# Block-sparse attention, Fourier mixing and an MLP in one kernel: from the tenth head pair on, DMAs turn q, k and the selection mask, and TensorE sums k's blocks

## The chip, the cores and the metric

The kernel runs on one core of one Trainium2 chip. Its time is the device time of one execution in microseconds. Before the change three runs gave 328.68, 330.34 and 330.57 us; the median is 330.34 us. Five engines work beside each other, each through its own instructions in order: TensorE (PE; its weight loads are PEld), VectorE (DVE), ScalarE (ACT), GpSimd (POOL) and SyncE (SP), which here only issues DMAs.

## The reference

Inputs are q, k and v of 4 batches, 8 heads, 768 positions and 64 channels, and two weight matrices. For each head the 768 keys form 12 blocks of 64. A query is scored against the mean key of each block (the gate), keeps the three best blocks that aren't in its future and its own block, and attends to their keys causally. The attention output goes through a two-dimensional Fourier transform over positions and channels, whose real part is added to it; then come a normalisation over the channels and an MLP.

```python
k_rep = k.reshape(B, H, n_blocks, block, D).mean(axis=3)
gate_scores = np.einsum('bhsd,bhnd->bhsn', q, k_rep)
gate_scores = np.where(causal, gate_scores, -1000000000.0)
top_idx = np.argsort(gate_scores, axis=-1)[..., -top_k:]
# mask: the three best blocks and the own block, and causal
scores = np.where(mask, scale * np.matmul(q, k.transpose(0, 1, 3, 2)), -1000000000.0)
out = softmax(scores) @ v
...
X = np.fft.fft(np.fft.fft(x, axis=1), axis=2)
u = x + np.real(X)
un = (u - mean(u)) / np.sqrt(var(u) + 1e-06)
return u + np.maximum(un @ w_ch1, 0.0) @ w_ch2
```

Only the order of the gate scores matters, but it must be right in float32, since a swapped block changes the output.

## The kernel before, in words

Work goes by pairs of heads: `kk` = 0 to 15, four pairs to a batch. Each pair has a slot of six parts (`p` = 0 to 5) in the main loop (L748 to L797). What a slot does for its own pair and for the next two is written out by hand: `USUAL` and `NORM` (L746, L747) name the part in which each stage stands. The order on TensorE and GpSimd is the program's order (`manual_schedule`, L679); a scheduler orders DVE, ACT and SP by its own estimate of when each instruction is ready.

The stages, by the lines that the prediction speaks of:

- `load_qk`, `load_v` (L213, L227): SP loads q, k and v of a pair, two DMAs each, some pairs ahead.
- `stage_A` (L266), in slot `kk` for pair `kk+2`: TensorE transposes q and k by 128x128 blocks in float32 (L281, 12 to a pair). Before pair 8 q goes to float32 (`qT`) and GpSimd casts it to the f16 operand `qg` (L242); from pair 8 on (`SPLIT`) ACT makes the f16 high part of 64 q (L289), DVE the remainder (L290), and GpSimd copies the high part. DVE sums k's columns by blocks (L294) and splits the sums in two f16 parts (L306, L307). ACT copies k to the f16 operand `kI` (L313).
- `stage_B` (L318), in part 5 of the same slot: the gates. Up to pair 7 five float32 matmuls (L325), from pair 8 on ten f16 ones (L333); then DVE adds the causal constants, finds the third largest of each row (L342) and writes the selection `gmp`.
- `stage_C` (L352), in part 3 of the slot after: TensorE transposes the selection (L356, five), DVE copies it to rows 64 to 75 of `qg` (L359). `kI` holds a constant in those rows (-60000 at a key's own block), so that the score matmul over 76 rows adds the mask.
- `stage_S` (L378): scores (L388) and exponential (L393), for both heads `e` and three sections `s` each: six to a slot, one to a part. From pair 7 on DVE masks the diagonal after it (L399).
- `stage_AV` (L401): output (L414) and division by the row sum (L419, L420).

After a batch's fourth pair its Fourier stages (`stage_S1`, L488 to L499; `stage_S2`, L515 to L529), the normalisation (`stage_N`, L545 to L562), a turn of its result (`stage_T`: SP's transposing DMA L570 for batches 1 and 2 and a part of 3, else TensorE L574) and the MLP (`stage_M1`, L589 to L594; `stage_M2`, L603 to L607) are put between the stages of later pairs as units by `filler` (L654), a planner that spreads units over the half parts by a credit. A unit of the Fourier chain stands where its due time by the planner's own clock (`feed.now`) says; that clock runs on the costs handed to `main` and on the units' costs. The last batch's chain and MLP have no pair left to stand beside; they make up the end.

PSUM tiles come from four buffers of one bank ("ps") and two of two banks for the scores ("sc").

In the profile a slot is the stretch from the first score matmul of its pair (L388) to that of the next.

Of the kernel before, what the change touches and what calls it, by code (L numbers as in the profile page):

```python
# [19 lines left out]
def _consts_np():  # L20
# [30 lines left out]
    IndN = np.where(nn[:, None] == (s[None, :] // 64), NEG, 0.0).astype(np.float16)  # L51
    return dict(CS=CS, SS=SS, CD=CD, SDN=SDN, SDP=SDP, ident32=ident32, ident16=ident16,
                ut01=ut01, ltri=ltri, cz24=cz24, oth24=oth24, IndN=IndN)
# [65 lines left out]
def kernel(  # L119
# [65 lines left out]
    kI_t = [[const([128, S], F16, f"kI_{e}_{sl}") for sl in range(3)] for e in range(2)]  # L185
    v16_t = [const([128, 2, NST, 66], F16, f"v16_{sl}") for sl in range(4)]
    qg_t = [[const([128, S], F16, f"qg_{e}_{sl}") for sl in range(3)] for e in range(2)]
    warm = const([128, 512], F16, "warm")
    kr24_t = [const([128, 2 * NB], FP, f"kr24_{sl}") for sl in range(2)]
    krx_t = [const([128, 2, 2 * NB], F16, f"krx_{sl}") for sl in range(2)]  # L190
# [11 lines left out]
    SPLIT = 8  # L202
# [32 lines left out]
    def cast_v(kk):  # L235
        P[kk]["v16"] = v16_t[kk % 4]
        nc.gpsimd.tensor_copy(out=v16_t[kk % 4][:, :, :, 0:64], in_=P[kk]["vn"])

    def cast_q(kk):
        d = P[kk]  # L240
        for e in range(2):
            nc.gpsimd.tensor_copy(out=d["qg"][e][0:64, :],  # L242
                                  in_=d["qt" if kk < SPLIT else "qh"][64 * e:64 * e + 64, :])

# [21 lines left out]
    def stage_A(kk, who, g):  # L266
        d = P[kk]
        src = d["qn"] if who == 0 else d["kn"]
        if who == 0 and g == 0:
            d["qt"] = apool.tile([128, S], FP, tag="qT32", name=f"qT32_{kk}")  # L270
            if kk >= SPLIT:
                parts = d["qt"].bitcast(F16)
                d["qh"], d["ql"] = parts[:, 0:S], parts[:, S:2 * S]
            d["qg"] = [qg_t[e][kk % 3] for e in range(2)]
        if who == 1 and g == 0:
            d["kI"] = [kI_t[e][kk % 3] for e in range(2)]
            d["kr12"] = spool.tile([128, NB], FP, tag="kr12", name=f"kr12_{kk}", bufs=2)
            d["kr24"] = kr24_t[kk % 2]
# [6 lines left out]
        if who == 0:  # L285
            if kk < SPLIT:
                (nc.scalar.copy if kk == LATE else nc.vector.tensor_copy)(out=d["qt"][:, cols], in_=flat)
            else:
                nc.scalar.activation(out=d["qh"][:, cols], in_=flat, func=AF.Copy, scale=QS)  # L289
                STT(out=d["ql"][:, cols], in0=flat, scalar=QS, in1=d["qh"][:, cols], op0=MULT, op1=SUB)  # L290
            if g == 1 and kk != LATE:
                cast_q(kk)
        else:
# [3 lines left out]
            if g == 1 and kk < SPLIT:  # L297
# [3 lines left out]
            elif g == 1:  # L301
                d["krx"] = krx_t[kk % 2]
                for e in range(2):
                    r, c = slice(64 * e, 64 * e + 64), slice(NB * e, NB * (e + 1))
                    hi, lo = d["krx"][r, 0, c], d["krx"][r, 1, c]
                    nc.vector.tensor_scalar(out=hi, in0=d["kr12"][r, :], scalar1=QS, scalar2=None, op0=MULT)  # L306
                    STT(out=lo, in0=d["kr12"][r, :], scalar=QS, in1=hi, op0=MULT, op1=SUB)  # L307
            for e in range(2):
                dst, src_ = d["kI"][e][0:64, cols], flat[64 * e:64 * e + 64]
                if kk < EARLY and g == 1 and e == 1:  # L310
                    nc.vector.tensor_copy(out=dst, in_=src_)
                else:
                    nc.scalar.copy(out=dst, in_=src_)  # L313

# [3 lines left out]
    def stage_B(kk):  # L318
# [9 lines left out]
        else:  # L328
            gps = pst([128, NG, 2, 2 * NB], f"g_{kk}")
            krx = d["krx"].rearrange("p o n -> p (o n)")  # L330
            for st in range(1, NST):
                for n, part in enumerate((d["qh"], d["ql"])):
                    nc.tensor.matmul(gps[:, st - 1, :, :].rearrange("p o n -> p (o n)"),  # L333
                                     part[:, 128 * st:128 * (st + 1)], krx, start=(n == 0), stop=(n == 1))
            nc.vector.tensor_tensor(out=gsf, in0=gps[:, :, 0, :], in1=cz24[:, 1:NST, :], op=ADD)
            nc.vector.tensor_tensor(out=gsf, in0=gps[:, :, 1, :], in1=gsf, op=ADD)
# [12 lines left out]
        else:  # L349
            STT(out=gm, in0=gm, scalar=QS, in1=oth24[:, 1:NST, :, :], op0=MULT, op1=MULT)  # L350

    def stage_C(kk):  # L352
# [5 lines left out]
        for e in range(2):  # L358
            nc.vector.tensor_copy(out=d["qg"][e][64:64 + NB, 128:S],  # L359
                                  in_=gt[32 * e:32 * e + NB].rearrange("p a c -> p (a c)"))  # L360
# [17 lines left out]
    def stage_S(kk, e, s):  # L378
        d = P[kk]
        if s == 0:  # L380
            d.setdefault("pt", {})[e] = apool.tile([128, 3 * SEC], F16, tag=f"ptl{e}",
                                                   name=f"ptl_{kk}_{e}")
# [3 lines left out]
        for (jt, a0, a1, co) in SECS[s]:  # L386
            diag = by_pe and a0 == 128 * jt
            nc.tensor.matmul(sp[:, co:co + (a1 - a0)],  # L388
                             d["kI"][e][0:76, 128 * jt:128 * (jt + 1)],
                             d["qg"][e][0:76, a0:a1], start=True, stop=not diag)  # L390
            if diag:
                nc.tensor.matmul(sp[:, co:co + 128], id16, ltri, start=False, stop=True)  # L392
        nc.scalar.activation(out=pt[:, SEC * s:SEC * (s + 1)], in_=sp[:, 0:SEC], func=AF.Exp,  # L393
                             scale=0.125 if kk < SPLIT else 0.125 / QS)
# [284 lines left out]
    with tc.manual_schedule(engines={mybir.EngineType.PE, mybir.EngineType.Pool}):  # L679
# [12 lines left out]
        for t in krx_t:  # L692
            nc.gpsimd.memset(t, 0.0)
        for t in gmp_t:
            nc.vector.memset(t, 0.0)
        for sl in range(3):
            for e in range(2):
                nc.gpsimd.dma_start(kI_t[e][sl][64:64 + NB, :], dr["IndN"].ap())
        nc.gpsimd.dma_start(ut01, dr["ut01"].ap())
        for e in range(2):  # L700
            for sl in range(3):
                nc.gpsimd.memset(qg_t[e][sl][64:64 + NB, 0:128], 0.0)
        load_v(0)
        for sl in range(4):
# [43 lines left out]
        for kk in range(NK):  # L748
            at = NORM if kk == NORM_SLOT else USUAL
            for p in range(6):  # L750
# [9 lines left out]
                if p == 1 and kk - 1 == NORM_SLOT:  # L760
                    main(stage_B, 0.35, kk + 1)
                if p == at["A1"] and kk + 2 < NK:
# [67 lines left out]
```

## Time and profile before

| what | value |
|---|---|
| three runs | 328.68, 330.34, 330.57 us |
| the profiled execution: its own time / its span | 330.56 us / 328.8 us |
| clock granted to TensorE, mean over the span | 0.995 |
| busy: PE, DVE, ACT, POOL | 309.1, 229.8, 179.9, 84.3 us |
| starts of slots 6 to 15 | 75.8, 86.9, 106.0, 124.8, 142.5, 162.1, 179.5, 197.6, 216.3, 234.5 us |
| last exponential of slot 15 | 249.6 us |
| longest total of PE's own waits with a named releaser | 3.4 us (scores on the exponential) |

How to read it. Times in a view are microseconds from the span's start; "L603" is line 603 of the kernel. The page gives each engine's busy time, the span in 40 slices of 8.2 us with the busy share in tenths, and the chain of work that ended last. A group line names line, engine, operation, out<-in, count, then busy time and mean duration in ns, then the idle time before it and who ended it. A mean duration holds the pipeline's depth: matmuls start one behind another at a fraction of it, and the chain of waits shows what each adds. SPq lines are the times in which SP issues a DMA. A wait line says who waited for whom, with total, count and longest.

### The profile page before, as it was taken

How to read it: one execution, taken by the hardware profiler on the slowest of the kernel's cores; microseconds unless marked ns; L12 is line 12 of the kernel's file. 1: busy time of each engine (PE TensorE's matmuls, PEld its weight loads, DVE VectorE, ACT ScalarE, POOL GpSimd, SP SyncE). 2: the span in 40 equal slices, each digit the busy share in tenths (PEclk: the TensorE clock that was granted, in tenths of full speed). 3: DMA queues.
4: the chain of work that ended last, by engine and by line, in shares of the span. 5: the costliest groups of instructions: out<-in, count | busy, mean ns of one | idle time of the engine just before them, and what ended most of it. 6: DMA issues, size and time to landing. Idle time of an engine off the chain costs nothing.

```text
span 328.8 us, 6922 instructions
## 1 busy us (share of the span) xinstructions
PE 309.1 (94%) x2656; PEld 199.5 (61%) x2656; DVE 229.8 (70%) x736; ACT 179.9 (55%) x276; POOL 84.3 (26%) x137
## 2 busy tenths in 40 slices
PE   7799998997799999998999999997999999999994
PEld 3577776976566667654666776553666654566442
DVE  3778879489786898998667889995357588433211
ACT  3178888598976766446595856345564302244000
POOL 8444573540464030505041131302030000000000
PEclk9999998899999999999999999999999999999999
DMA  8995989992499642434733000114100011200021
GB/s 201 244 260 135 268 129 227 155 208 50 98 181 202 114 98 50 140 85 114 190 76 74 0 2 35 45 53 96 66 0 2 0 67 70 90 3 0 34 96 64
DMA packets 92929, 33.02 MB, mean 100 GB/s; under 512 B 85352, under 2 KB 88752, under 8 KB 92896
## 3 DMA queue, kind: packets, MB, share of 16 engines
q1 hardware_dynamic: 87600, 27.71, 34.5%
q0 software_dynamic: 3552, 4.40, 8.8%
q10 hardware_dynamic: 1744, 0.46, 0.6%
q8 instruction: 21, 0.34, 0.4%
q14 instruction: 12, 0.10, 0.1%
HBM read 28.63 MB, written 6.29 MB: 106 GB/s over the span
## 4 chain that ended last, share of the span: by engine, by line
PE 68%; DVE 19%; ACT 7%; DMA 2%; issue 2%; ACTq 0%; DVEq 0%
PE ch L603 19%; PE ha L589 15%; PE hb L589 8%; PE sc L388 7%; PE av L414 4%; ACT ptl L393 3%; ACT kI L313 3%; PE g L325 3%; PE za L488 2%; PE tp L281 2%; DVE mx L342 2%; DVE kr L294 2%; DVE bst L528 2%; DVE ptl L399 2%; DVE u L526 2%
## 5 line engine op out<-in xcount | busy, mean ns | idle before, releaser
L393 ACT ACTIVATE ptl<-sc 128x896 f16<-128x896 f32 x96 | 87.3, 918 | 43.9 <-PE sc L388 34.4
L603 PE MATMUL ch<-w_sb,hT 128*128 128x512 f16 x384 | 91.2, 379 | 0.9 <-DVE qT L290 0.9
L589 PEld LDWEIGHTS <-w_sb 128*128 128x128 f16 x512 | 48.6, 97 | 37.7 <-issue 3.8
L589 PE MATMUL ha<-unT,w_sb 128*128 128x512 f16 x256 | 65.7, 379 | 0.6 <-DMA unT<-x 0.5
L603 PEld LDWEIGHTS <-hT 128*128 128x128 f16 x384 | 36.4, 97 | 36.3 <-issue 0.8
L388 PE MATMUL sc<-qg,kI 76*128 76x512 f16 (+3 forms) x256 | 55.0, 307 | 3.4 <-ACT ptl L393 3.4
L592 ACT ACTIVATE hT<-ha 128x512 f16<-128x512 f32 x64 | 38.1, 598 | 30.7 <-PE ha L589 30.5
L594 DVE TENSOR_SCALAR hT<-hb 128x256 f16<-128x256 f32 x64 | 26.7, 420 | 30.3 <-PE hb L589 30.2
L589 PE MATMUL hb<-unT,w_sb 128*128 128x256 f16 x256 | 38.4, 272 | 1.7 <-DMA unT<-x 1.6
L434 POOL TENSOR_TENSOR fs<-x 128x384 f16<-128x384 f16 x12 | 10.9, 909 | 106.7 <-DVE x L420 91.9
L388 PEld LDWEIGHTS <-kI 76*128 76x128 f16 x256 | 24.1, 100 | 19.5 <-issue 2.6
L313 ACT CAST kI<-tp 64x384 f16<-64x384 f32 x57 | 27.0, 474 | 14.6 <-DVE kr L294 13.5
L606 DVE TENSOR_TENSOR u<-ch,u 128x512 f32<-128x512 f32 x24 | 16.4, 683 | 19.6 <-PE ch L603 19.3
L414 PEld LDWEIGHTS <-ptl 128*128 128x128 f16 x672 | 24.1, 97 | 3.1 <-DVE ptl L399 0.4
L414 PE MATMUL av<-v,ptl 128*128 128x65 f16 x672 | 25.7, 193 | 0.1
L294 DVE TENSOR_REDUCE kr<-tp 128x6 f32<-128x384 f32 x32 | 17.0, 549 | 8.2 <-PE tp L281 8.0
L561 ACT ACTIVATE x<-u,nmr,rstd 128x512 f16<-128x512 f32 x12 | 8.9, 804 | 18.8 <-issue 17.0
L392 PE MATMUL sc<-ltri,id 128*128 128x128 f16 x84 | 18.6, 222 | 0.0
L420 DVE TENSOR_TENSOR x<-av,rcp 128x384 f16<-128x384 f32 x32 | 17.8, 556 | 1.0
L399 DVE TENSOR_TENSOR ptl<-ptl,ut 128x384 f16<-128x384 f16 x36 | 13.8, 419 | 5.7 <-ACT ptl L393 5.7
L528 DVE BATCH_NORM_STATS2 bst<-u 128x6 f32<-128x512 f32 x24 | 16.6, 692 | 1.2 <-ACT u L524 0.7
L359 DVE COPY qg<-gt 12x640 f16<-12x640 f16 x32 | 15.5, 484 | 2.0 <-PE gt L356 1.1
(115 smaller groups left out, 408.2 us busy)
## 6 DMA issues: line engine op xcount, KB each, us to landing
vn<-in_v_dram SPq DMA_DIRECT2D x32, 192.0 KB, 3.6
out_dram<-u SPq DMA_DIRECT2D x24, 256.0 KB, 2.0
kn<-in_k_dram SPq DMA_DIRECT2D x30, 192.0 KB, 3.4
qn<-in_q_dram SPq DMA_DIRECT2D x30, 192.0 KB, 3.3
w_sb<-in_moe_w_ch_dram POOLq DMA_DIRECT2D x8, 256.0 KB, 7.0
w_sb<-in_moe_w_ch_dram POOLq DMA_DIRECT2D x4, 512.0 KB, 8.8
cs_sb<-c_CS SPq DMA_DIRECT2D x1, 289.5 KB, 4.6
ss_sb<-c_SS SPq DMA_DIRECT2D x1, 289.5 KB, 4.8
```

Source lines behind the costliest of these rows:

```text
L294: nc.vector.tensor_reduce(out=d["kr12"][:, 6 * g:6 * g + 6], in_=ps.rearrange("p a (x c) -> p a x c", x=2), axis=mybir.AxisListType.X, op=ADD)
L313: nc.scalar.copy(out=dst, in_=src_)
L388: nc.tensor.matmul(sp[:, co:co + (a1 - a0)], d["kI"][e][0:76, 128 * jt:128 * (jt + 1)], d["qg"][e][0:76, a0:a1], start=True, stop=not diag)
L392: nc.tensor.matmul(sp[:, co:co + 128], id16, ltri, start=False, stop=True)
L393: nc.scalar.activation(out=pt[:, SEC * s:SEC * (s + 1)], in_=sp[:, 0:SEC], func=AF.Exp, scale=0.125 if kk < SPLIT else 0.125 / QS)
L399: nc.vector.tensor_tensor(out=dg, in0=dg, in1=um, op=MULT)
L414: nc.tensor.matmul(av[:, st, 0:65], pt[:, o:o + 128], d["v16"][:, e, jt, 0:65], start=(cnt == 0), stop=(cnt == 20))
L528: nc.vector.bn_stats(out=bst, in_=u_b[:, kt, :])
L589: nc.tensor.matmul(hp_, w1_sb[:, dt, 128 * it:128 * (it + 1)], unT[:, dt, c0:c1], start=(dt == 0), stop=(dt == NDT - 1))
L592: nc.scalar.activation(out=hT[:, c0:c1], in_=hp_, func=AF.Relu)
L594: nc.vector.tensor_scalar(out=hT[:, c0:c1], in0=hp_, scalar1=0.0, scalar2=None, op0=mybir.AluOpType.max)
L603: nc.tensor.matmul(cps, x["hT"][it][:, 128 * st:128 * (st + 1)], w2_sb[:, it, :], start=(it == 0), stop=(it == NIT - 1))
```

## The change

It sets `SPLIT` to 9 and replaces the path of pairs 9 to 15, in three steps.

1. `split(kk+2)`, where `stage_A` of q stood (part 2): from the loaded float32 q and k, ACT writes the high f16 part of 64 q and 64 k (two instructions over 768 columns), DVE the remainders (640 and 768 columns), all with positions on the partitions. Two transposing DMAs of 12 blocks of 128x128 each, on SP, turn q's two parts into `qhl` and k's high part with the constant rows into `kI`. There are no transposes on TensorE for these pairs, no block sums on DVE and no copies of q on GpSimd.
2. `stage_R(kk+2)`, where `stage_B` stood (part 5): 24 matmuls of two columns, with 64-column weights from k's high and low part and an indicator as the moving operand, sum k's blocks in PSUM. DVE splits the sums in two f16 parts, ACT copies both to partitions 64 to 127.
3. `stage_B(kk+1)` moves to part 1 of the slot after, with ten f16 matmuls of 24 columns. DVE writes the selection into the low part's columns of `qs`, and a third transposing DMA turns `qs` into `qg`, mask rows included. `stage_C` goes.

Pair 8 goes back to the float32 path. `kI` and `qg` hold both heads in one tile with 128-column blocks of the two in turn; `v16` has three buffers in place of four, the exponentials' tiles one per head in place of two. In slot 3 SP loads the constant columns and GpSimd clears the unused ones. The costs that `main` hands the planner follow (transposes 1.4 less to a slot, gates 0.3, block sums 0.6).

```diff
-    SPLIT = 8
+    SPLIT = 9
...
+    def turn(dst, src):
+        nc.sync.dma_start_transpose(dst.rearrange("p s e c -> p (s e) c"),
+                                    src.rearrange("p s e c -> p (s e c)"))
+
+    def split(kk):
+        d = P[kk]
+        kn, qn = d["kn"], d["qn"]
+        d["qs"] = qs = qs_t[kk % 2]
+        d["qhl"] = apool.tile([128, S], FP, tag="qT32", name=f"qhl_{kk}").bitcast(F16).rearrange(
+            "p (s e c) -> p s e c", e=2, c=128)
+        khi, qhi = ks[:, :, :, 0:64], qs[:, :, :, 0:64]
+        nc.scalar.activation(out=qhi, in_=qn, func=AF.Copy, scale=QS)
+        STT(out=qs[:, 1:NST, :, 64:128], in0=qn[:, 1:NST, :, :], scalar=QS, in1=qhi[:, 1:NST, :, :],
+            op0=MULT, op1=SUB)
+        turn(d["qhl"], qs)
+        nc.scalar.activation(out=khi, in_=kn, func=AF.Copy, scale=QS)
+        turn(kI_t[kk % 3], ks)
+        STT(out=klo, in0=kn, scalar=QS, in1=khi, op0=MULT, op1=SUB)
+        d["kI"], d["qg"] = kI_t[kk % 3], qg_t[kk % 3]
+
+    def stage_R(kk):
+        d = P[kk]
+        d["krs"] = krs = krs_t[kk % 2]
+        rps = pst([64, 2, NB], f"r_{kk}")
+        for st in range(NST):
+            for e in range(2):
+                o = rps[:, e, 2 * st:2 * st + 2]
+                nc.tensor.matmul(o, ks[:, st, e, 0:64], ind2, start=True, stop=False)
+                nc.tensor.matmul(o, klo[:, st, e, :], ind2, start=False, stop=True)
+        hi, lo = krs[0:64, :, 0, :], krs[0:64, :, 1, :]
+        nc.vector.tensor_copy(out=hi, in_=rps)
+        nc.vector.tensor_tensor(out=lo, in0=rps, in1=hi, op=SUB)
+        nc.scalar.copy(out=krs[64:128, :, :, :], in_=krs[0:64, :, :, :])
...
-            gps = pst([128, NG, 2, 2 * NB], f"g_{kk}")
-            krx = d["krx"].rearrange("p o n -> p (o n)")
+            gps = pst([128, NG, 2, 2, NB], f"g_{kk}")
             for st in range(1, NST):
-                for n, part in enumerate((d["qh"], d["ql"])):
-                    nc.tensor.matmul(gps[:, st - 1, :, :].rearrange("p o n -> p (o n)"),
-                                     part[:, 128 * st:128 * (st + 1)], krx, start=(n == 0), stop=(n == 1))
+                for e in range(2):
+                    nc.tensor.matmul(gps[:, st - 1, e, :, :].rearrange("p o n -> p (o n)"),
+                                     d["qhl"][:, st, e, :],
+                                     d["krs"][:, e, :, :].rearrange("p o n -> p (o n)"), start=True, stop=True)
...
-            STT(out=gm, in0=gm, scalar=QS, in1=oth24[:, 1:NST, :, :], op0=MULT, op1=MULT)
+            STT(out=d["qs"][:, 1:NST, :, 64:64 + NB], in0=gm,
+                scalar=QS * QS, in1=oth24[:, 1:NST, :, :], op0=MULT, op1=MULT)
+            turn(qg_t[kk % 3], d["qs"])
...
-                if p == 1 and kk - 1 == NORM_SLOT:
-                    main(stage_B, 0.35, kk + 1)
-                if p == at["A1"] and kk + 2 < NK:
+                if p == 1 and (kk - 1 == NORM_SLOT or SPLIT <= kk + 1 < NK):
+                    main(stage_B, 0.3 if kk + 1 >= SPLIT else 1.05, kk + 1)
+                if p == at["A1"] and kk + 2 < min(SPLIT, NK):
                     main(stage_AA, 0.7, kk + 2, 1)
-                if p == at["C"] and kk + 1 < NK:
+                if p == at["C"] and kk + 1 < min(SPLIT, NK):
                     main(stage_C, 0.3, kk + 1)
...
                 if p == at["A0"]:
                     if kk + 2 < NK:
-                        main(stage_AA, 0.7, kk + 2, 0)
+                        if kk + 2 < SPLIT:
+                            main(stage_AA, 0.7, kk + 2, 0)
+                        else:
+                            split(kk + 2)
...
                 if p == at["B"] and kk + 2 < NK:
-                    main(stage_B, 1.05 if kk + 2 < SPLIT else 0.35, kk + 2)
+                    if kk + 2 < SPLIT:
+                        main(stage_B, 1.05, kk + 2)
+                    else:
+                        main(stage_R, 0.6, kk + 2)
...
+            if kk == 3:
+                nc.gpsimd.memset(ks[:, :, :, 64 + NB:128], 0.0)
+                for t in qs_t:
+                    nc.gpsimd.memset(t[:, 0, :, 64:128], 0.0)
+                for e in range(2):
+                    nc.sync.dma_start(ks[:, :, e, 64:64 + NB],
+                                      dr["IndT"].ap().rearrange("(st p) n -> p st n", p=128))
+                    nc.gpsimd.memset(ind2[:, e:e + 1], 0.0)
+                    nc.gpsimd.memset(ind2[64 * e:64 * e + 64, e:e + 1], 1.0)
```

## The prediction

> **What bounds the kernel now.** I read the page first: busy shares, slices and chain of all engines.
>
> ```profile
> PE 309.1 (94%) x2656; PEld 199.5 (61%) x2656; DVE 229.8 (70%) x736; ACT 179.9 (55%) x276; POOL 84.3 (26%) x137
> PE   7799998997799999998999999997999999999994
> DVE  3778879489786898998667889995357588433211
> PE 68%; DVE 19%; ACT 7%; DMA 2%; issue 2%; ACTq 0%; DVEq 0%
> ```
>
> TensorE is full from the twelfth slice (about 90 us) on, and the chain runs through it for 68%; DVE holds 19%. So work taken off TensorE counts, unless another queue ends the same stretch. That is read by slots, from the busy time per stretch (PE, PEld, DVE, ACT, POOL in us).
>
> ```profile
> 124.76:142.51 17.75, 17.75 (x155) 11.13 (x154) 16.66 (x47) 9.18 (x14) 4.43 (x5) 1.00 0.37 97
> 142.51:162.13 19.62, 18.77 (x151) 10.78 (x149) 15.45 (x59) 10.93 (x17) 4.41 (x5) 1.00 0.51 124
> 197.61:216.32 18.71, 17.91 (x154) 11.12 (x153) 17.75 (x53) 8.41 (x13) 4.26 (x5) 1.00 0.11 43
> 216.32:234.52 18.20, 16.07 (x124) 8.62 (x123) 11.99 (x44) 8.99 (x12) 1.78 (x2) 1.00 0.34 87
> ```
>
> These are slots 9, 10, 13 and 14. In 9 and 13 DVE is at 94 and 95%, as full as TensorE. Slot 14 has 2 us of idle TensorE. Now the chain of waits (start, length, what) around slots 6, 11 and 12 gives what each stage adds to a full TensorE.
>
> ```profile
> 74.29 1.04 PE g L325 x10
> ...
> 162.68 0.66 PE tp L281 x6
> ...
> 172.33 0.39 PE gt L356 x5
> ...
> 175.81 0.64 PE av L414 x21
> ...
> 178.13 0.25 PE g L333 x10
> ```
>
> Last the queue that gets the most new work, SP, and the two waits of TensorE that the change touches: the view of the tile that DMAs transpose ("turn" below), SP's timeline, TensorE's timeline, the waits.
>
> ```profile
> L570 SPq DMA_TRANSPOSE unT<-x x14: 1195/1218/1289, 150.2 to 279.2; - x14
> DMA to landing us min/median/max: 2.4/2.4/3.2
> ```
>
> ```profile
> 150.25 7.85 SPq L570 DMA_TRANSPOSE unT<-x  x6
> 158.19 1.12 SPq L224 DMA_DIRECT2D qn<-in_q_dram  x2
> 159.40 0.49 SPq L607 DMA_DIRECT2D out_dram<-u  x1
> ```
>
> ```profile
> 80.59 0.40 PE L574 MATMUL unt<-id,x 128*128 128x128 f16 x4 [1.56 <-DVE x L557]
> ```
>
> ```profile
> PE hb L589 <- DMA unT<-x: 1.6, 1, 1.6
> PE ch L603 <- DVE qT L290: 0.9, 1, 0.9
> ```
>
> A transposing DMA of four 128x128 blocks keeps SP for 1.22 us and lands 2.4 us after its start; six stand in a row for 7.85 us.
>
> **The sum.** It starts from the profiled execution's own 330.56 us (span 328.8), 0.22 above the median of 330.34.
>
> *TensorE's work.* Per pair 9 to 15 two transposing stages go (2 x 0.66) and the mask's (0.39): -1.71. Ten gate matmuls stay; at 48 columns they add 0.25, and at 24 I leave that. The 24 block-sum matmuls are new: two columns moving, 64 columns of weights. Their nearest rows are L333 (0.025 each), L414 (0.64 / 21 = 0.030) and L356 (0.39 / 5 = 0.078, of which the first one's start is a part; inside it starts follow at 0.056). So 24 x 0.025 to 0.056 is 0.6 to 1.34. L356's weights are 44 columns and load in 0.102, L333's 128 in 0.096; narrow weights cost a few ns. I take 0.029, or 0.70. Net -1.01, times 7 is -7.1. Pair 8 goes back from 0.25 to the 1.04 to 1.10 of L325: +0.85. Sum -6.2 (from -6.9 to -1.7).
>
> The Trainium skill ("TensorE: Matmul & The Clock Gate", LDWEIGHTS) says a load takes its columns divided by 1.2 ns, which is an estimated 53 ns for 64 columns and 1.28 us a pair, and would give back 4.1 us. The 44-column loads of L356 hide behind 128 moving columns, so no row here excludes it.
>
> *What of it isn't on the path, slots 6 and 7.* In the built program's order the scheduler places pair 9's remainders early: DVE's 768-column one between the last statistics and L545, the 640-column one between L548 and L551. Both stand in the normalisation chain for which TensorE idles 1.56 us. By L528 (512 columns in 0.59 to 0.60 on the chain) they cost 0.86 + 0.72. ACT's new high part of pair 10 falls mostly in its 0.6 us wait at 83.7 (+0.2); its two q copies ahead of the last turn's copy go (0.77), and a score section (0.38) now stands before the first MLP unit: +0.6. Pair 9's k transposes (0.66) stood before that unit too, so their gain doesn't reach the end. Together +1.2 (0 if DVE's order fits a gap, 2.3 if nothing is absorbed).
>
> *Slots 10 and 11, SP.* Slot 10 is where SP meets the six turns of batch 1. A 12-block turn: between the 1.22 of the 4-block one and three times that, 3.66. A plain output DMA takes 0.36, so 0.215 a block, and I take 0.36 + 12 x 0.215 = 2.9. From issue's end to landing a 4-block turn needs 1.2; three times the bytes take 1.2 to 3.6, I take 2.4. In the built order SP runs pair 12's q and k turns, an output, k's loads, then the six turns, an output, a q load, and only then pair 11's mask turn, without which slot 11's first scores can't start. The six wait for the normalisation, which started its turns 7.7 us into slot 10. With DVE lighter by the term below I put them at 5.7; SP itself is free at about 5.5 (pair 12's k turn can't start before its high part, near 0.8, + 2.9, outputs and loads 1.5). They end at 13.6, the mask turn starts at 14.5 and lands 5.3 later, at 19.8. TensorE's slot 10 shrinks from 18.4 of work to about 17.4. Stall 2.4 (0 if the normalisation is 2.5 earlier; 4.3 if it is as late as before). I take +2.2. All of DVE's selection of pair 11 is done by about 10, behind that queue.
>
> *Slots 13 and 14.* DVE sheds per pair two sums (0.47 each), two remainders (0.47), four small splits (0.18) and two mask copies (0.48), 3.6 us; it gains 0.72 + 0.86 and two small ones (0.2): 2.0. Net -1.6 us, so where DVE is as full as TensorE (slot 13) 1.0 more than this isn't to be had. Slot 14's first MLP unit waits for the six turns anyway (1.6 above), so what TensorE saves there is partly spent waiting. +1.2 (0 to 2.3).
>
> *Idle that goes.* The wait of 0.9 on DVE's q remainder (L290) has no cause left: -0.9 (0 to -1.7, with 0.8 of L515's wait on DVE).
>
> Hidden, at nothing: ACT has 4 to 10 us free in every slot from 7 on and trades 2.9 for about 1.9 us a pair; if it is late, exponentials are, and TensorE next. It waits for TensorE's block sums before it may overwrite `ks`, and an exponential stands behind that; the two score buffers cover a microsecond. GpSimd loses 2 x 0.87 a pair; the memsets of slot 3 fall in its waits (91.9 us for L420 in all). The tighter `ptl` and `v16` buffers are freed by stages that stand earlier in TensorE's order than the new writers. SP's outputs and loads wait behind the turns, but loads are some pairs ahead. The last batch's end, from 250 us, is untouched.
>
> -6.2 + 1.2 + 2.2 + 1.2 - 0.9 = -2.5: **328.0 us**.
>
> **The rivals.**
>
> 1. *The cover holds* (normalisation early enough, the mask turn lands before slot 11, DVE's inserts half hidden): -6.2 + 0.6 - 0.9 = -6.5, 324.0 us. For it: SP's other slots have 12 us of new and old work to 17. Against: 7.85 us of turns in one row directly ahead of the mask turn.
> 2. *Narrow weights cost 0.056 each*: 24 x 0.027 x 7 = +4.5, so 332.5 us. For it: L356's spacing. Against: L356's spacing is that of its 128 moving columns. This is the skill's load rule above.
> 3. *SP becomes the bound; slower.* A pair needs three 12-block turns of T, six loads (0.48 each) and about an output: 3 T + 3.3. From T = 4.4 us this is over a slot's 16.5, and the mask turns of all pairs fall behind. At T = 5, 1.8 x 6 slots, and slots 10 and 14 lose some 2 us each more: about 338 to 340 us. For it: proportional cost is 3.66, and no row shows a turn of this size. Against: 24 blocks in 7.85 us are 0.33 each, or 3.9 for 12.
>
> The Trainium skill ("VectorE: DVE Perf Modes", The three transpose paths, and its rules for kernel authors) speaks for rival 3: it gives 1309 ns to a 128x128 transpose by DMA and 390 ns to TensorE's, and prefers TensorE where PSUM can take the result. At 36 blocks a pair that would be an estimated 47 us of a 17 us slot. The 0.33 us a block of this trace doesn't agree with it.
>
> **How the numbers follow.** My forecast 0.42 (326 to 330.5), rival 1 0.28 (322 to 326), rival 2 0.12, rival 3 0.18. The range 322.5 to 334.0 holds the first three nearly whole and leaves out rival 3. About 1% of 330.34, 3.3 us, is what a measurement can tell from no change, so faster means below 327.0 and slower above 333.6. Faster: all of rival 1 and a fourth of my own, 0.38. Slower: rival 3 and a part of rival 2, 0.22. The rest, 0.40, is within 1%.
>
> **What would show it.** TensorE: 24 `r` matmuls a pair at 0.025 to 0.030 each (0.056 is rival 2); no transposes of pairs 9 to 15. SP: 12-block turns of 2.7 to 3.7 us (over 4.4 is rival 3), landing 5 to 6 after the start. Slot 11's first score matmul waits 1 to 4 us for the DMA that writes `qg` (no wait is rival 1); the wait before L574's successor in slot 6 grows from 1.56 to about 3. Slot 13 is near 17, DVE still full there. Wrong would be a new wait of TensorE on `krs` or `qhl`, or a slot 15 that waits for its mask as slot 11 does.

## The result, and the profile after

Four runs of the changed kernel gave 347.43, 354.19, 354.63 and 356.68 us, median 354.41, beside 330.45 for the kernel before in the same session. The ratio is 1.059, with a 95% interval of 1.046 to 1.072: clearly slower, where 328.0 was forecast with 322.5 to 334.0 as the range. The ratio is made from the 347.43 and a fifth run of 351.87 us; the others, in which TensorE's granted clock was lower still (0.936 to 0.949), are left out of it, so gains below are given by ratios or from lowest run to lowest. The profiled execution is the one of 347.43 us (span 345.6, clock 0.954).

The page of the changed kernel: busy shares, TensorE's slices (8.6 us each here), the granted clock, the DMA share.

```profile
PE 315.0 (91%) x2705; PEld 199.9 (58%) x2705; DVE 217.3 (63%) x691; ACT 172.7 (50%) x253; POOL 71.7 (21%) x126
PE   8799998996999929999589699999899999999995
PEclk9989999998999985999879789999999999999999
DMA  9999999993999978477897414442700011300021
```

TensorE's row has holes that the row of before doesn't have: a 2 in the fifteenth slice, a 5 in the twentieth, a 6 in the twenty-third. Right behind the first two the clock row falls, to 5 and to 7. DVE, ACT and GpSimd all have less to do than before, so none of them is a bound by its work. Which stretch lost the time is read by slots (columns as in the prediction: PE, PEld, DVE, ACT, POOL, clock, DMA share, GB/s). Slots 8, 10, 11, 13 and 14 after:

```profile
106.84:132.92 26.08, 19.24 (x184) 12.98 (x182) 14.79 (x47) 13.54 (x21) 1.14 (x3) 0.87 0.97 173
150.78:170.69 19.91, 17.47 (x155) 9.42 (x152) 11.77 (x45) 7.39 (x10) 2.68 (x3) 1.00 0.87 178
170.69:198.36 27.67, 22.09 (x173) 12.99 (x174) 14.73 (x45) 15.72 (x24) 3.46 (x5) 0.81 0.75 128
217.33:233.37 16.04, 16.04 (x158) 9.90 (x157) 14.40 (x44) 5.86 (x8) 2.56 (x3) 1.00 0.45 101
233.37:251.33 17.96, 16.69 (x135) 9.06 (x133) 11.76 (x43) 9.19 (x13) 1.78 (x2) 1.00 0.45 110
```

and slots 8 and 11 of the kernel before:

```profile
106.00:124.80 18.80, 18.49 (x181) 12.90 (x177) 16.96 (x56) 12.88 (x22) 3.63 (x5) 1.00 0.51 101
162.10:179.50 17.40, 17.40 (x159) 11.46 (x158) 12.35 (x46) 13.07 (x22) 5.32 (x7) 1.00 0.44 105
```

Slot 8 is 7.3 us longer and slot 11 10.3 us. All the rest adds up to -0.8, slot 13 alone to -2.7. The span grew by 16.8, so two slots explain it. What the change was to save is there all the same: TensorE was busy for 26.0 of its 315.0 us at half clock (3.4 of 309.1 before); with these counted half, its work fell from 307.4 to 302.1 us, by an estimated 5.3. But it idles for 30.6 us in place of 19.7, and the half clock costs 13.0 in place of 1.7. Who waits in the two slots is in the waits (total, count, longest):

```profile
ACT qs L320 <- DMA qg<-qs: 22.4, 5, 7.7
DVE qs L321 <- ACT qs L320: 20.7, 5, 7.6
PE ya L524 <- DVE x L452: 6.8, 1, 6.8
PE unt L606 <- DVE x L589: 2.9, 1, 2.9
PE sc L420 <- DMA qg<-qs: 2.4, 1, 2.4
```

The first two are new, and no line of the prediction has them. L320 is ACT's high part in `split(kk+2)`. It writes into `qs_t[kk % 2]`, and the mask turn of the pair that had this buffer two pairs ago reads the buffer: the write must wait for it. ACT's timeline at the end of slot 8 shows where the write stands:

```profile
118.52 0.60 ACT L624 ACTIVATE hT<-ha 128x512 f16<-128x512 f32 x1
126.56 0.84 ACT L320 ACTIVATE qs<-qn 128x768 f16<-128x768 f32 x1 [7.44 <-DMA qg<-qs]
127.31 0.57 ACT L529 CAST yT<-ya 128x386 f16<-128x386 f32 x1
```

This is pair 11's high part. The program calls it in part 2 of slot 9; the scheduler has put it into slot 8, behind its fifth exponential, where pair 9's mask turn has not even been issued. Behind it, ready, stand ACT's copies of the Fourier stage; DVE's remainder (L321) waits for ACT and holds up DVE's division (L452), whose result TensorE needs. The Trainium skill ("PSUM — Partial Sum Buffer", Engine vs sequencer instructions) calls the queues of ScalarE and VectorE strict FIFOs. The trace agrees: 7.44 us without an instruction on ACT.

The same stretch in four pieces, for the clock:

```profile
113.00:119.60 6.60, 6.60 (x62) 4.36 (x61) 6.09 (x23) 4.91 (x7) 0.98 (x3) 1.00 1.09 205
119.60:126.40 6.80, 2.34 (x26) 1.92 (x23) 0.19 (x1) 0.00 (x0) 0.00 (x0) 1.00 1.12 214
126.40:136.60 10.20, 7.82 (x46) 4.46 (x47) 5.16 (x12) 5.58 (x9) 0.00 (x0) 0.50 0.69 141
136.60:146.00 9.40, 9.40 (x82) 5.54 (x81) 8.63 (x30) 3.22 (x4) 2.55 (x3) 1.00 0.36 91
```

TensorE runs dry at 121.94 and idles for 6.8 us, the wait of L524 above. The clock falls to half at 126.4, while it still idles, and stays there for 10.2 us. The 7.82 us that TensorE is busy there would be an estimated 3.9 at full clock (four matmuls of L635 take 1.91 us there and 1.03 just behind it). So the stall costs 6.8 and 3.9, 10.7 us in all; in the kernel with both edits below, which has neither, slots 8 and 9 together are 10.6 us shorter. Slot 11 has two such stalls: pair 13's write holds ACT for 7.65 us up to 170.99, just ahead of the slot, and pair 14's for 3.9 us up to 191.80, inside it; TensorE idles for 2.4 to 2.7 us at a time there, and 6.8 us at half clock go with each.

Pair 11's mask turn, for which pair 13's write waits, is issued at 165.65 behind six `unT` turns, as the prediction says. Why the mask turn of pair 9 came so late is in SP's timeline of slots 7 and 8:

```profile
94.23 9.20 SPq L310 DMA_TRANSPOSE qhl<-qs  x1
103.53 3.74 SPq L232 DMA_DIRECT2D kn<-in_k_dram  x2
107.31 7.91 SPq L232 DMA_DIRECT2D qn<-in_q_dram  x2
115.26 1.66 SPq L240 DMA_DIRECT2D vn<-in_v_dram  x2
117.08 2.47 SPq L310 DMA_TRANSPOSE kI<-ks  x1
119.66 1.12 SPq L232 DMA_DIRECT2D kn<-in_k_dram  x2
120.87 1.07 SPq L240 DMA_DIRECT2D vn<-in_v_dram  x2
122.05 2.44 SPq L310 DMA_TRANSPOSE qg<-qs  x1
```

A turn that takes 1.41 us to issue later on takes 9.20 here, and the loads behind it up to 4.5 each. Beside them run GpSimd's four loads of the second MLP weight (issued from 92.05 to 99.65, landing 7 to 16 us later). GpSimd's issues of them, two to a line, after and before:

```profile
92.05 1.54 POOL L269 DMA_DIRECT2D w_sb<-in_moe_w_ch_dram  x2
98.89 1.52 POOL L269 DMA_DIRECT2D w_sb<-in_moe_w_ch_dram  x2
```

```profile
91.14 1.55 POOL L261 DMA_DIRECT2D w_sb<-in_moe_w_ch_dram  x2
100.57 1.54 POOL L261 DMA_DIRECT2D w_sb<-in_moe_w_ch_dram  x2
```

The kernel before has these loads at nearly the same times, though the change ties the last two to another instruction (k of pair 9 loaded, in place of DVE's remainder of q, L290). New are the turns beside them: before, SP needed at most 1.2 us for a load there.

### The profile page after: what moved, and what is told of

Read it like the earlier page. It is cut to its first block, busy times and chain, and to the rows that moved or that the text cites. A ratio compares the mean times of both kernels' runs of the same rounds, so it can differ in the third digit from the quotient of the medians.

```text
span 345.6 us, 7004 instructions
## 1 busy us (share of the span) xinstructions
PE 315.0 (91%) x2705; PEld 199.9 (58%) x2705; DVE 217.3 (63%) x691; ACT 172.7 (50%) x253; POOL 71.7 (21%) x126
## 5 line engine op out<-in xcount | busy, mean ns | idle before, releaser
L635 PE MATMUL ch<-w_sb,hT 128*128 128x512 f16 x384 | 91.5, 384 | 0.0
L621 PEld LDWEIGHTS <-w_sb 128*128 128x128 f16 x512 | 50.0, 100 | 45.5 <-issue 12.8
L621 PE MATMUL ha<-unT,w_sb 128*128 128x512 f16 x256 | 68.8, 393 | 4.1 <-DVE u L638 2.4
L420 PE MATMUL sc<-qg,kI 76*128 76x512 f16 (+3 forms) x256 | 56.9, 316 | 5.8 <-ACT ptl L425 3.4
L635 PEld LDWEIGHTS <-hT 128*128 128x128 f16 x384 | 36.9, 98 | 37.9 <-issue 1.1
L621 PE MATMUL hb<-unT,w_sb 128*128 128x256 f16 x256 | 39.7, 279 | 3.1 <-ACT hT L624 2.7
L420 PEld LDWEIGHTS <-kI 76*128 76x128 f16 x256 | 25.0, 103 | 23.2 <-issue 4.9
L424 PE MATMUL sc<-ltri,id 128*128 128x128 f16 x84 | 18.8, 224 | 0.0
L321 DVE SCALAR_TENSOR_TENSOR qs<-qn,qs 128x640 f16<-128x640 f32 x7 | 5.8, 824 | 20.7 <-ACT qs L320 20.7
L593 ACT ACTIVATE x<-u,nmr,rstd 128x512 f16<-128x512 f32 x12 | 8.9, 804 | 18.6 <-issue 17.0
L452 DVE TENSOR_TENSOR x<-av,rcp 128x384 f16<-128x384 f32 x32 | 17.7, 553 | 0.7
L307 ACT CAST kI<-tp 64x384 f16<-64x384 f32 x29 | 13.7, 474 | 7.6 <-DVE kr L295 6.7
L320 ACT ACTIVATE qs<-qn 128x768 f16<-128x768 f32 x7 | 5.9, 843 | 22.4 <-DMA qg<-qs 22.4
L250 POOL CAST qg<-qT 64x768 f16<-64x768 f32 x18 | 14.8, 820 | 10.9 <-DVE qT L291 9.9
```

What stands on the lines that cost most here:

```text
L250: nc.gpsimd.tensor_copy(out=d["qg"][0:64, :, e, :], in_=d["qt"][64 * e:64 * e + 64, :].rearrange("p (s c) -> p s c", c=128))
L420: nc.tensor.matmul(sp[:, co:co + (a1 - a0)], d["kI"][0:76, jt, e, :], d["qg"][0:76, a0 // 128:a1 // 128, e, :], start=True, stop=not diag)
L452: nc.vector.tensor_tensor(out=x_b[:, :, 64 * h:64 * h + 64], in0=av[:, :, 0:64], in1=rcp.to_broadcast([128, NST, 64]), op=MULT)
L621: nc.tensor.matmul(hp_, w1_sb[:, dt, 128 * it:128 * (it + 1)], unT[:, dt, c0:c1], start=(dt == 0), stop=(dt == NDT - 1))
L635: nc.tensor.matmul(cps, x["hT"][it][:, 128 * st:128 * (st + 1)], w2_sb[:, it, :], start=(it == 0), stop=(it == NIT - 1))
```

## The experiments

Theory A: the write into `qs` waits for the mask turn, at a place where ACT, DVE and then TensorE stand behind it. Theory B: the weight's loads make the turns of slot 7 late. Theory C: SP's order (mask turn of pair 11 behind six `unT` turns, the prediction's term). Rival: the turns are late because SP or the DMAs are the bound (the prediction's third rival). The length of each slot in the profiles, in us:

| slot | before | after | third `qs` | order | loads early | both | both, TensorE turns batch 1 |
|---|---|---|---|---|---|---|---|
| start of 6 | 75.8 | 75.4 | 76.0 | 74.8 | 76.5 | 75.0 | 75.4 |
| 6 | 11.1 | 12.9 | 13.7 | 12.3 | 12.6 | 12.2 | 12.2 |
| 7 | 19.1 | 18.5 | 27.1 | 18.3 | 20.2 | 18.1 | 18.1 |
| 8 | 18.8 | 26.1 | 18.2 | 22.8 | 17.8 | 17.3 | 17.3 |
| 9 | 17.7 | 17.9 | 16.0 | 18.0 | 16.0 | 16.0 | 17.8 |
| 10 | 19.6 | 19.9 | 20.7 | 22.4 | 20.4 | 21.7 | 17.7 |
| 11 | 17.4 | 27.7 | 27.5 | 20.7 | 27.2 | 20.1 | 18.5 |
| 12 | 18.1 | 19.0 | 18.9 | 17.3 | 18.9 | 17.3 | 17.7 |
| 13 | 18.7 | 16.0 | 16.0 | 16.0 | 16.0 | 16.0 | 16.9 |
| 14 | 18.2 | 18.0 | 17.9 | 18.0 | 17.9 | 18.0 | 17.9 |
| 15 and the end | 94.3 | 94.3 | 94.3 | 94.3 | 94.3 | 94.3 | 94.2 |
| the profiled run | 330.56 | 347.43 | 348.28 | 336.60 | 339.78 | 327.70 | 325.33 |
| median of the runs | 330.45 | 354.41 | 354.61 | 336.52 | 340.26 | 327.75 | 325.74 |

The kernel before, run on the same chip each time, had 329.65 us beside "third `qs`", "order" and "loads early", 328.98 beside "both" and 329.2 beside the last. "Third `qs`" to "both, TensorE turns batch 1" are the kernels told of below.

**A third buffer for `qs`.**

```diff
-    qs_t = [const([128, NST, 2, 128], F16, f"qs_{sl}") for sl in range(2)]
+    qs_t = [const([128, NST, 2, 128], F16, f"qs_{sl}") for sl in range(3)]
...
-        d["qs"] = qs = qs_t[kk % 2]
+        d["qs"] = qs = qs_t[kk % 3]
```

> A third buffer for qs; everything else as in the changed kernel. Theory A (ACT and DVE stand still because the next high part must not overwrite qs before the mask turn has read it): the waits of ACT on the turn qg<-qs (22.4 us, five times) and of DVE behind it (20.7) fall below 3 us together, slots 8 and 11 shrink from 26.1 and 27.7 us to 18 to 21, the half clock after them goes, and the time falls from 354 to 330 to 338. Rival (SP or the DMAs themselves are too slow, the bound that the prediction called its third rival): the turns are late whatever the buffer, TensorE's scores now wait for qg in place of ACT, and the time stays above 345.

The third buffer also takes in two constants of the early part, last read at 89 us. Measured: 354.61 us (348.28 to 357.75), nothing gained: slot 8 falls to 18.2 as expected, slot 11 stays at 27.5, and slot 7 grows to 27.1. Read hastily this speaks for the rival. The waits of this kernel and ACT's timeline at the end of slot 10 say otherwise:

```profile
ACT qs L320 <- DMA qg<-qs: 15.4, 4, 8.2
ACT qs L320 <- DMA qn<-in_q_dram: 6.7, 1, 6.7
```

```profile
162.77 0.92 ACT L425 ACTIVATE ptl<-sc 128x896 f16<-128x896 f32 x1 [1.13 <-PE sc L420]
171.88 0.84 ACT L320 ACTIVATE qs<-qn 128x768 f16<-128x768 f32 x1 [8.19 <-DMA qg<-qs]
```

The wait is still ACT's, not TensorE's. The write at 171.88 is now pair 14's; in the changed kernel pair 14's stood a slot later. With a buffer more the scheduler places each write a slot earlier, into the next wait; pair 11's moved up into slot 7, where it waits for its load (6.7 us) and makes slot 7 27.1 us long. My number was wrong, because I had taken the order as fixed.

**The same wait taken away by order.** Two buffers, but the write is queued behind the first exponential of its own slot.

```diff
-        nc.scalar.activation(out=qhi, in_=qn, func=AF.Copy, scale=QS)
+        with tc.issue_after(P[kk - 2]["exp", 0, 0].ins):
+            nc.scalar.activation(out=qhi, in_=qn, func=AF.Copy, scale=QS)
```

> Two buffers of qs as in the changed kernel, but ACT's high part of pair kk+2 is queued behind the first exponential of slot kk, which itself needs pair kk's turned mask. Theory A: ACT can't wait there, because the turn that it would wait for has landed before the exponential's scores could start; the time is that of three buffers within 4 us, 330 to 340. If ACT's wait was only a sign of turns that are late anyway, the time stays above 345. The split of q comes later than with three buffers, so qhl and the block sums come later: TensorE may wait for qhl or krs by up to 2 us a slot.

Measured: 336.52 us (330.57 to 340.97), 17 less from lowest to lowest, by one added order. No wait of ACT or DVE on `qs` is left. The turns are as late as they were, and now TensorE itself shows it (the lines of this kernel are one higher; the stretches are slots 8 and 10):

```profile
PE sc L421 <- DMA qg<-qs: 9.2, 2, 5.3
```

```profile
105.42:128.18 22.76, 17.41 (x184) 12.05 (x182) 15.10 (x47) 13.24 (x21) 1.14 (x3) 0.94 1.14 202
146.18:168.56 22.38, 17.64 (x155) 9.35 (x152) 14.83 (x49) 10.48 (x14) 2.68 (x3) 0.95 0.83 149
```

So both are true: the turns are late (5.3 us in slot 8, 3.9 in slot 10), and the write's place made more of it than TensorE's own wait for the mask would have.

**The weight's loads after slot 5**, with the write where the scheduler puts it.

```diff
-            if kk in (6, 7):
-                pool_after(P[kk + 2]["qt"] if kk + 2 < SPLIT else P[kk + 2]["kn"][:, 0, 0, :])
-                load_w2(2 * kk - 12)
-                load_w2(2 * kk - 11)
+            if kk == 5:
+                pool_after(P[kk + 2]["qt"])
+                for c in range(4):
+                    load_w2(c)
```

> The four loads of the second MLP weight go one and two slots earlier (after slot 5), so that they don't run beside the turns of slot 7; qs keeps two buffers. Theory B (slot 8's stall begins with the q turn of pair 10, which SP needed 9.2 us to issue beside these loads, and which pushed the mask turn of pair 9 to 122 us): that turn is issued in 1.4 to 3 us, the mask turn of pair 9 lands before 116, slot 8 falls from 26.1 to 18 to 20 us, and slot 11 keeps its 27: 7 to 10 us less in all, about 345. Theory A without B: ACT's 7.4 us wait in slot 8 stays at 5 or more, and the time stays at 350 to 355.

Measured: 340.26 us, ratio 1.034 (1.025 to 1.043) to the kernel before. SP's line for pair 10's q turn, and slots 8 and 11:

```profile
100.89 2.69 SPq L310 DMA_TRANSPOSE qhl<-qs  x1
```

```profile
109.34:127.11 17.77, 17.43 (x185) 11.99 (x183) 13.64 (x45) 13.05 (x20) 1.14 (x3) 1.00 0.71 109
163.58:190.80 27.22, 21.95 (x172) 13.00 (x173) 14.74 (x45) 15.72 (x24) 3.45 (x5) 0.81 0.69 128
```

The turn takes 2.69 in place of 9.20 us, slot 8 is below that of the kernel before, slot 11 is untouched. Theory B holds for slot 8 and for it alone. One smaller point missed: the mask turn of pair 9 was issued only at 117.56, though ACT then waits for it no longer than 0.95 us. The gain is 8 us by the ratios (1.059 to 1.034), within the 7 to 10 expected. Slot 11 is the same stall with another cause of lateness, six `unT` turns.

**The layout alone**: all pairs on the float32 path, with the change's tiles, buffers and planner's costs.

```diff
-    SPLIT = 9
+    SPLIT = 16
```

> All pairs on the float32 path of the first pairs (no split, no block sums on TensorE, no turns of q, k and mask); what stays of the change is its layout (kI and qg of two heads in one tile, v16 with three buffers, one tile for each head's exponentials, the costs of the planner). Against the kernel before, eight pairs have float32 gates in place of f16 ones, 8 x 0.85 us more on TensorE (the prediction's price). If the layout and the buffers are harmless: 335 to 339. If the tighter buffers cost by themselves, 342 or more.

Measured: 335.14 us, 5.5 above the 329.65 of the kernel before (ratio 1.017, 1.010 to 1.024). If the float32 gates of eight pairs are all of that, they are 0.69 each. TensorE's work, with half clock counted half as above, grew from 307.4 to 313.6 us, which is 0.77 each. So the gates alone explain it, and the layout and the tighter buffers cost nothing that shows.

**Both edits**, order and loads.

> The two edits that helped together: the high part of q behind the slot's first exponential, and the second MLP weight's loads after slot 5. If the stalls of slot 8 have two causes in a row (the loads delay the turns, ACT waits for the late turn), slot 8 falls from 22.8 us (order alone) to 17.5 to 19, and the time from 336.5 to 329 to 333. What stays is slot 10, whose end waits for pair 11's mask turn behind six unT turns (22.4 us with the order alone). If the edits treat the same loss twice, the time stays at 335 to 337.

Measured: 327.75 us, ratio 0.999 (0.996 to 1.002): no change from the kernel before that a measurement can tell. Slots 8, 9, 10 and 13 of this kernel, and SP in slot 10:

```profile
105.39:122.64 17.25, 17.25 (x184) 12.05 (x182) 14.14 (x46) 12.88 (x20) 1.14 (x3) 1.00 0.94 139
122.64:138.68 16.04, 16.04 (x157) 9.90 (x156) 14.65 (x43) 6.95 (x10) 2.55 (x3) 1.00 0.90 181
138.68:160.35 21.67, 17.63 (x155) 9.32 (x152) 14.74 (x49) 10.49 (x14) 2.68 (x3) 1.00 0.78 152
197.65:213.69 16.04, 16.04 (x158) 9.90 (x156) 15.13 (x45) 6.59 (x9) 2.55 (x3) 1.00 0.57 125
```

```profile
145.24 9.22 SPq L603 DMA_TRANSPOSE unT<-x  x6
154.55 0.53 SPq L640 DMA_DIRECT2D out_dram<-u  x1
155.14 0.42 SPq L232 DMA_DIRECT2D qn<-in_q_dram  x1
155.65 2.48 SPq L310 DMA_TRANSPOSE qg<-qs  x1
```

In slots 8, 9 and 13 TensorE is busy without a gap, with SP carrying all the turns; SP is not the bound, and the third rival falls. From lowest run to lowest the edits gain 17 and 8 us alone and 20 together, since both treat slot 8. What stays is slot 10: DVE has finished pair 11's selection at 149.85, its turn is issued at 155.65, and slot 11's scores wait 4.0 us.

**The block sums twice**, on top of both edits (the sums are computed a second time into the same tile).

```diff
-        for st in range(NST):
+        for st in [st for _ in range(2) for st in range(NST)]:
```

> As the kernel with both edits, but the block sums are computed twice into the same tile (48 in place of 24 matmuls a pair; the output is the same). If the matmul stream is what a slot lasts, 24 x 7 more cost 0.031 each as the trace's spacing shows: +5.2 us. If narrow weights cost 0.056 (the prediction's second rival), +9.4. If the slots are set by something else than TensorE's work (SP, ACT's order), +0 to 2.

Measured: 332.1 us, ratio 1.010 (1.004 to 1.017) after 0.999, some 4 us more. The slots that have no gap grow by 0.76 each, 9 and 13 shown:

```profile
123.38:140.18 16.80, 16.80 (x182) 10.66 (x181) 14.66 (x43) 6.87 (x10) 2.55 (x3) 1.00 0.85 173
198.71:215.51 16.80, 16.80 (x182) 10.66 (x181) 15.16 (x44) 6.49 (x9) 2.55 (x3) 1.00 0.50 119
```

0.76 / 24 is 0.032 a matmul. Slot 10, which waits for something else, took none of it (21.3 after 21.7). The second rival falls.

**Pair 11's mask turn ahead of three `unT` turns**, on top of both edits. The diff shows the core; the planner's unit also waits for pair 11's gates.

```diff
+            if b == 1 and st >= 3:
+                with tc.issue_after(P[11]["mturn"].ins):
+                    nc.sync.dma_start_transpose(dst, x["x"][:, st, :])
```

> As the kernel with both edits, and SP issues the mask turn of pair 11 after three of batch 1's six unT turns, in place of after all six (the units of these turns stand behind pair 11's gates in the program). Theory C (the prediction's +2.2 term for slots 10 and 11): the scores of slot 11 wait under 1 us for qg in place of 3 to 4, slot 10 falls from 22 to 18 to 19.5, and the time by 2 to 4 us, to 326 to 329. Rival: what slot 10 gains, the MLP of batch 1 loses because its operand is turned later, and the time is that of both edits within 1 us.

Measured: 329.22 us, ratio 1.000 (0.997 to 1.004), slot 10 22.6 us. The rival of this run is right. The scores' wait is gone from the list, and in its place stands

```profile
PE ha L626 <- DMA unT<-x: 5.0, 2, 4.0
```

The MLP of batch 1 needs the `unT` turns as urgently as slot 11 needs the mask. This order doesn't help; the next runs take turns away from that stretch.

**TensorE transposes batch 1's result**, three of the six row groups or all, on top of both edits.

```diff
-    TURNED = ((), range(NST), range(NST), (0, 1))
+    TURNED = ((), (), range(NST), (0, 1))
```

> As the kernel with both edits, but SP turns three of the six row groups of batch 1's normalised result and TensorE the other three, so that pair 11's mask turn stands behind three turns in place of six. If SP's queue alone makes slot 11's scores wait (4.2 us), the wait falls under 1 us; TensorE gets 12 transposes (some 1.2 us, by 0.10 each from batch 0's) and the time falls by 2 to 3.5, to 324.5 to 326. If DVE is what is late there (the selection of pair 11 and the normalisation stand in one queue), the wait moves to TensorE's transposes or to the first MLP unit and the time stays at 327 to 329.

> As the kernel with both edits, but TensorE transposes all of batch 1's normalised result and SP none of it: no turn stands ahead of pair 11's mask turn. TensorE has 24 transposes more, about 2.4 us. If SP's queue alone is the cause, slot 11's wait is gone and the time is 325.5 to 327; against three turns on each it shows what of the wait DVE's selection still makes. If DVE is the cause, 328 to 330.

Measured: three on each 329.85 us (1.001, 0.998 to 1.004), outside of both ranges; all on TensorE 325.74 us, ratio 0.987 (0.982 to 0.993), as expected and faster than the kernel before. Slots 10 and 14 of the first, and its longest wait of TensorE on a DMA:

```profile
140.61:158.73 18.12, 17.27 (x161) 9.79 (x160) 13.92 (x49) 9.80 (x14) 2.75 (x3) 1.00 0.90 193
210.46:229.35 18.89, 12.21 (x110) 6.76 (x108) 10.71 (x41) 7.61 (x9) 1.78 (x2) 0.95 0.45 105
```

```profile
PE sc L421 <- DMA qg<-qs: 6.7, 1, 6.7
```

Slot 10 does what was expected in both (18.1 and 17.7 us, no wait for the mask), so Theory C is right about the cause. With three on each the planner then has no MLP work left for slot 14 (12.2 us of TensorE's work in 18.9), where the mask turn of pair 15 stands behind batch 2's six turns: the same wait as in slot 11, one batch later and without cover. The gain of slot 10 goes there and into the end (the span from slot 15 on is 100.2 in place of 94.3).

**Pair 9's remainder of k behind the normalisation**, on top of both edits; then with three row groups on TensorE, and with all six.

```diff
+            with tc.issue_after(X[0]["normed"].ins):
+                STT(out=klo, in0=kn, scalar=QS, in1=khi, op0=MULT, op1=SUB)
```

> As the kernel with both edits (327.75), and DVE's remainder of k of pair 9 (0.93 us, which stands between batch 0's last statistics and its normalisation) is held behind the normalisation. The prediction's term for slots 6 and 7 says that such an insert is on the chain for which TensorE waits: the wait ahead of batch 0's transposes falls from 2.5 to about 1.6 us, slot 6 from 12.2 to 11.3, the time by 0.7 to 1. If DVE's order has gaps there or the planner gives the gain back, 0 to 0.3.

> Both edits, the remainder of k of pair 9 behind the normalisation, and three of batch 1's six row groups transposed on TensorE. If the two last edits help each in its own slot, their gains add: 323.5 to 325.5, 1.0 to 1.6% under the kernel before. If they don't, it is the better of the two, 326 to 328.

> The best version so far (both edits, batch 1's result transposed on TensorE, 325.74 us, 0.987 of the kernel before) with the remainder of k of pair 9 behind the normalisation as well. Slot 6 falls from 12.2 to 11.1 us, slot 7 gives some 0.4 back: 0.7 us less, 325.0, or 0.984 to 0.986 of the kernel before. If the planner of batch 1 reacts as in the combination before, 327 to 330.

Measured: 328.4, 330.86 and 325.32 us; ratios 0.996 (0.992 to 1.000), 1.003 (1.000 to 1.006) and 0.990 (0.987 to 0.994). The second is outside of both its ranges, as it has the long end of three on each; the third's ratio stays above the 0.984 to 0.986 expected. Slot 6 is 11.06 us and slot 7 18.6 in all three. With the insert they are 11.75 and 18.6 in the run with the mask turn moved ahead, and 12.2 and 18.1 with both edits alone, where 3.4 us at half clock fall into slot 6. So the insert stood on the chain as the prediction says, with 0.7 us. That is too little for these intervals, and the total leaves it open. The last kernel is about 1% faster than the one before.

## Why the prediction was wrong

**The step that failed** is the paragraph "Hidden, at nothing". It looked for what ACT's new instructions wait for and named the block sums, before `ks` may be overwritten; that wait is small (2.9 us in four, with both edits). It didn't ask the same of `qs`, whose reader is a DMA that itself stands behind SP's queue, and it took ACT's free time as cover ("ACT has 4 to 10 us free in every slot"). Free time doesn't cover an instruction that waits at the head of a queue. The second step that failed is the price of a turn on SP: one figure, 2.9 us, stood for all of them, and only slots 10, 11 and 14 were asked for what stands beside. The weight's loads of slot 7, there before the change too, made one turn take 9.2, and pair 9's mask late. Together the two steps cost some 20 us (ratio 1.059 to 0.999). That these cause it is shown by the order run and the loads run. The half clock that a stall brings stood in no term either.

**What was right.** With these two stalls out, the kernel takes 327.75 us, where the sum gave 328.0. That is nearer than it should be: beside the 328.98 of the kernel before in its own session it is 1.2 less, where the sum had 2.5, and the ratio can't be told from 1. Part of the agreement is luck, as the terms missed in both directions: slots 10 and 11 came out 4.7 us longer than before, where the sum has about 0.2, and slot 13 2.7 shorter. The terms:

- TensorE's work, -6.2: -5.3 in the changed kernel and -5.7 with both edits, half clock counted half. This holds.
- Block sums 0.029 each: 0.032 measured by doubling. The 24-column gates still follow at 0.025. The load rule of the Trainium skill ("TensorE: Matmul & The Clock Gate", LDWEIGHTS), 0.053, is not borne out by these matmuls.
- Pair 8 back on float32, +0.85: 0.69 to 0.77 by the layout run.
- Slots 6 and 7, +1.2: together 1.3 longer in the changed kernel, where the wait ahead of the transposes of slot 6 grew from 1.56 to 2.9 (about 3 was said); with both edits the wait is 2.2 and the two slots only 0.2 longer.
- Slots 10 and 11, SP, +2.2: right, in its parts too. In the changed kernel the six turns start 5.9 us into slot 10 (5.7 was said), the mask turn starts at 14.9 (14.5) and lands at 19.9 (19.8), and slot 11's scores wait 2.4. A 12-block turn with nothing beside it takes only 1.41 to 1.45 us to issue and lands 3.7 after its start, but this one took 3.08 and 5.0 (2.9 and 5.3 were taken). With both edits the wait is 4.0, since the six turns start 6.6 us into the slot and take 9.2.
- Slots 13 and 14, +1.2: wrong for 13. It fell by 2.7 us, more than TensorE's 1.0; its busy time went from 17.9 to 16.0, so the planner also put other units there. DVE has 14.4 us of work in it and was no limit.
- Idle that goes, -0.9: right, TensorE waits for no remainder of q any more.

**The chances.** Slower had 0.22, by rivals 2 and 3. Rival 2 fell. Rival 3's condition, a turn of over 4.4 us, was met once (9.2), but by the traffic beside it and not by its size; the other turns took 1.4 to 3.1. (Its terms add up to some 341 to 343 us rather than 338 to 340.) ACT's wait stood in no rival. The range was too narrow because no bound was put on an engine that waits at the head of its queue, nor on a turn beside the weight's loads.

**What stays open.** That a turn's issue takes 9.2 us beside the weight's loads was shown by moving the loads; what in the queues is full was not. That the half clock follows from a stall is read from the order in time; it wasn't tried apart from the stall, and a stall's length doesn't settle it: 2.2 us of idle TensorE in slot 6 brought 3.4 us at half clock with both edits, 3.1 us in slot 10 brought none with the block sums doubled.

## What to carry to other kernels

For each instruction that a change adds, ask what it must wait for (the last reader of its output buffer too, above all a DMA), where the scheduler will put it, and who stands behind it in that engine's queue; idle time of the engine is no answer. A buffer more may only let the scheduler place the same wait earlier, while an explicit order behind an instruction that can't start before the reader is done takes it away. When a stretch loses more than one wait, undo them one at a time and together: here 17 and 8 were 20.

## What the runs showed of the hardware

- A stall of TensorE can cost more than its length: in slot 8 6.8 us of idle time, and an estimated 3.9 lost to the half clock that came with it. The stretches at half clock inside the changed kernel are 3.4, 3.4, 10.2, 6.8 and 6.8 us long. The Trainium skill ("TensorE: Matmul & The Clock Gate", What's actually happening) says that the clock halves after an idle window of about 3.4 us and comes back after one of work. The trace agrees in the lengths, all multiples of 3.4; in the idle time it doesn't, as the longest gap ahead of the two of 6.8 us is 2.7 us.
- Three times the blocks in one transposing DMA cost little more to issue (1.43 us after 1.22), and 3.7 in place of 2.4 us to land, where nothing runs beside it.
- The same DMA took SP 9.2 us to issue beside GpSimd's weight loads, and everything behind it on SP waited as long; with these loads earlier it took 2.69.
- A matmul with two moving columns and 64 columns of weights follows the one before by 0.032 us, although its weight load is recorded at 0.113.
